# Loading the q weights ahead of the first K tile, and moving the first softmax ahead of a K tile's second turn

## The chip, the cores and the metric

The kernel runs on one core of one Trainium2 chip. The metric is the device time of one execution in microseconds (us); lower is better.

## The reference, cut to what matters

One decode step of a transformer block: layer norm, attention over the last 4096 positions of a cache (4 batches, 32 q heads on 16 K/V heads of width 128), output projection, then layer norm and a gated MLP.

```
q = xn @ wq                                  # 576 x 4096
scores = q @ K^T / sqrt(128);  p = softmax(scores);  o = p @ V
h = x + o @ wo;  h2 = h + (relu(gate) * up) @ W_down
```

K and V are 64 MB each in the window (a MB of a tile or of one load is 2^20 bytes here); with the weights 159.6 million bytes have to be read. There is little arithmetic per byte.

## The kernel before

K and V come in 16 tiles each, of 4 MB (128 partitions x 16384 bf16), into four slots of on-chip memory. One engine (SP) issues all these loads, in order. A load into a used slot first waits for the last reader of what lies there:

```python
def add_kv(kind, g):
    s = ring_slot(); off = slot0 + s * TILE
    place((kind, g), off, TILE, ("QK", g, 1) if kind == "K" else ("PV", g), ...)  # who must be done before the slot is reused
...
add_kv("K", 0)
place(("wq", 0), ...)            # q weights, a slot of their own; then 0.5 MB more of them
for g in range(1, NTILE):
    add_kv("K", g)
    if g >= 4:
        add_kv("V", g - 4)
```

So the queue is K0, wq, K1, K2, K3, K4, V0, K5, V1, K6, V2, K7 and so on. With four slots, K6 goes where K4 was: SP issues it when the scores of K4 are done.

A K tile is used in two halves. (QK stands for the matmuls that make the scores, PV for those of p @ V.) VectorE (DVE) turns a half (transposes it) in place, then TensorE (PE) makes 16 matmuls of 128x512 of it. There are two forms of the turn. The short form takes 4.4 us and its matmuls start every 0.43 us. The long form (`by_head`) takes 7.4 us and its matmuls start every 0.216 us at the full clock, 0.43 us at half of it.

```python
def do_k(g):                                  # after K4 the scores of batch 0 are complete
    if g: turn_k(g, 0)
    ...
    if g: turn_k(g, 1)
    if g == 4:
        row_max(0); pe_qk(g, 0, range(3)); head_max(0); pe_qk(g, 0, range(3, 4))
        exps(0); put_q(2)
    else:
        pe_qk(g, 0)
    ...                                       # g == 5: PV of V0 comes here
    pe_qk(g, 1)                               # frees the slot
```

Of the kernel before, what the change touches and what calls it, by code (L numbers as in the profile page):

```python
# [6 lines left out]
ALU = mybir.AluOpType  # L7
AX = mybir.AxisListType
# [12 lines left out]
NTILE = B * KVH // 4  # L21
# [6 lines left out]
BIG = 1e30  # L28


def by_head(g, w):
    return (g, w) in ((0, 0), (0, 1), (2, 1), (3, 1), (4, 1))


ENGS = ("sync", "scalar", "vector", "gpsimd", "tensor")
# [85 lines left out]
def bass_sequential_preLN__sliding_block_cached__glu_gated_reglu__decode_kernel(  # L121
# [12 lines left out]
    with ExitStack() as es:  # L134
# [7 lines left out]
        dve = lambda name, fn, deps=(): P.op("vector", name, fn, deps)  # L142
        act = lambda name, fn, deps=(): P.op("scalar", name, fn, deps)
        pool = lambda name, fn, deps=(): P.op("gpsimd", name, fn, deps)
# [6 lines left out]
        ident_f = sb("ident_f", [128, 128], FP32)  # L151
# [4 lines left out]
        c_am = sb("c_am", [128, 4, 16, 2], FP32)  # L156
# [5 lines left out]
        am = sb("am", [128, 4], FP32)  # L162
        msk = sb("msk", [128, 4], FP32)
# [75 lines left out]
        def add_kv(kind, g):  # L239
            b, qd = divmod(g, 4)  # L240
            s = ring_slot()
            off = slot0 + s * TILE
            cache = A_k_cache if kind == "K" else A_v_cache
            src = cache[b, 4 * qd:4 * qd + 4, SK - WIN:SK, :].rearrange("a (p t) d -> p a (t d)", p=32)
            place((kind, g), off, TILE, ("QK", g, 1) if kind == "K" else ("PV", g),
                  lambda e: e.dma_start(out=arena[:, off:off + TILE], in_=src), key=f"slot{s}")
# [5 lines left out]
        def last_rows(W):  # L252
            return W[512:576, :].rearrange("r (a n) -> (r a) n", a=2)

        add_kv("K", 0)
        s = ring_slot()
        wq_off = slot0 + s * TILE
        place(("wq", 0), wq_off, TILE, "QMM",
              lambda e: e.dma_start(out=arena[:, wq_off:wq_off + TILE], in_=main_rows(A_wq)), key=f"slot{s}")
        P.dma("sync", ("L", "wq", 1), lambda e: e.dma_start(out=pT[:, 0:2048], in_=last_rows(A_wq)), "d_wq1")  # L260
        for g in range(1, NTILE):
            add_kv("K", g)
            if g >= 4:
                add_kv("V", g - 4)
# [17 lines left out]
        for j in range(4):  # L282
            wd_off.append(off)
            for r0, r1 in ((0, 9),) if j < 3 else ((0, 6), (6, 9)):
                place(("wd", j, r0), off + r0 * D, (r1 - r0) * D, "DOWN",
                      lambda e, off=off, j=j, r0=r0, r1=r1: e.dma_start(  # L286
                          out=arena[:, off + r0 * D:off + r1 * D],
                          in_=B_W_down[j * 1152:(j + 1) * 1152, :].rearrange("(p r) n -> p (r n)", p=128)[:, r0 * D:r1 * D]))
# [5 lines left out]
                                                compare_op=ALU.not_equal, fill=1.0, base=0, channel_multiplier=1), ["c_idb0"])  # L294

        pool("c_xnT", lambda e: e.memset(xnT[:, :, :], 0.0))
        pool("c_idf0", lambda e: e.memset(ident_f[:, :], 0.0))
        pool("c_idf", lambda e: e.affine_select(out=ident_f[:, :], in_=ident_f[:, :], pattern=[[-1, 128]],
                                                compare_op=ALU.not_equal, fill=1.0, base=0, channel_multiplier=1), ["c_idf0"])
        pool("c_m40", lambda e: e.memset(c_m4[:, :, :], 0.0))  # L300
        pool("c_m41", lambda e: e.affine_select(out=c_m4[:, :, :], in_=c_m4[:, :, :], pattern=[[-1, 4], [-4, 32]],
                                                compare_op=ALU.not_equal, fill=1.0, base=0, channel_multiplier=1), ["c_m40"])
        pool("c_qW", lambda e: e.memset(arena[:, 0:2 * QWW].bitcast(FP32), 0.0))  # L303
        pool("c_am0", lambda e: e.memset(c_am[:, :, :, :], 0.0))
        pool("c_am1", lambda e: e.affine_select(out=c_am[:, :, :, :], in_=c_am[:, :, :, :], pattern=[[-2, 4], [-8, 16], [-1, 2]],
                                                compare_op=ALU.not_equal, fill=1.0, base=0, channel_multiplier=1), ["c_am0"])
# [7 lines left out]
                                                in_=c_qm[:, :, :].rearrange("p q (h j) -> p q h j", j=4),  # L314
# [20 lines left out]
        for q in range(4):  # L335
# [7 lines left out]
        dve("c_par0", lambda e: e.tensor_tensor(out=par[:, 0:1], in0=m4[:, 0:1], in1=m4[:, 2:3], op=ALU.add), ["c_m4"])  # L343
        dve("c_par", lambda e: e.tensor_scalar(out=par[:, 1:2], in0=par[:, 0:1], scalar1=-1.0, scalar2=1.0,
                                               op0=ALU.mult, op1=ALU.add), ["c_par0"])
        dve("c_am", lambda e: e.tensor_reduce(out=am[:, :], in_=c_am[:, :, :, :].rearrange("p a m s -> p a (m s)"), axis=AX.X, op=ALU.max),
            ["c_am1"])
        dve("c_msk", lambda e: e.tensor_scalar(out=msk[:, :], in0=am[:, :], scalar1=-1.0, scalar2=BIG, op0=ALU.add, op1=ALU.mult), ["c_am"])


        act("warm_sqrt", lambda e: e.activation(out=warm[:, 0:1], in_=eps_c[:, :], func=ACT.Sqrt), ["c_eps"])
# [64 lines left out]
        def put_q(b):  # L416
            for i in range(4):
                act(("QW", b), lambda e, i=i: e.copy(  # L418
                    out=bass.AP(tensor=arena, offset=32 * i * AW + b % 2 * QWW + 32 * i, ap=[[AW, 32], [128, 4], [514, 16], [1, 2]]),
                    in_=bass.AP(tensor=q_keep, offset=b * 128, ap=[[512, 32], [32, 4], [2, 16], [1, 2]])),  # L420
                    ["qkeep", "c_qW", ("QK", 4 * b - 5, 1) if b >= 2 else None] if i == 0 else [])


        def turn_k(g, w):
            k = arena[:, land[("K", g)] + w * QWW:][:, 0:QWW].bitcast(FP32)
            if by_head(g, w):
                dst = k.rearrange("p (n a k) -> p n k a", a=4, k=8)
                src = k.rearrange("p (n k a) -> p n k a", a=4, k=8)
            else:
                dst = k.rearrange("p (n h l a) -> p n l h a", h=2, l=2, a=2)  # L430
                src = k.rearrange("p (n l h a) -> p n l h a", h=2, l=2, a=2)
            dve(("TRA", g, w), lambda e: e.transpose(out=dst, in_=src), [("L", "K", g)] if w == 0 else [])  # L432


        def pe_qk(g, w, heads=range(4)):
            b, qd = divmod(g, 4)
            for a in heads:
                for cb in range(4):
                    first = a == cb == 0
                    deps = []  # L440
                    if first:
                        deps.append(("TRA", g, w))
                        if qd == 0 and w == 0:
                            deps.append(("QW", b))
                            if b >= 2:
                                deps += [("EXP", b - 2, 1), ("MAX", b - 2)]
                    sub, steps = (16 * a, [[2, 8]]) if by_head(g, w) else (a // 2 * 8 + a % 2 * 2, [[16, 4], [4, 2]])
                    off = land[("K", g)] + w * QWW + cb // 2 * 64 + sub + cb % 2
                    wo_ = b % 2 * QWW + (4 * qd + a) * 512 + cb * 128
                    pe(("QK", g, w), lambda e, off=off, steps=steps, wo_=wo_, qd=qd, first=first, last=a == cb == 3: e.matmul(  # L450
                        bank[SB[b % 2] + w], lhsT=arena[:, wo_:wo_ + 128],
                        rhs=bass.AP(tensor=arena, offset=off, ap=[[AW, 128], [128, 64]] + steps),
                        start=(qd == 0 and first), stop=(qd == 3 and last), skip_group_check=True), deps)
# [14 lines left out]
        def exps(b):  # L468
            pe(("MB", b), lambda e: e.matmul(m_ps[:, 0:1], lhsT=gm4[0:1, :], rhs=scl[0:1, 0:1], start=True, stop=True), [("GM1", b), "c_scl"])  # L469
            dve(("NB", b), lambda e: e.tensor_tensor(out=stat[:, b, 1:5], in0=msk[:, :],  # L470
                                                     in1=bass.AP(tensor=psb, offset=7 * 512, ap=[[4096, 128], [0, 4]]), op=ALU.add),
                [("MB", b), "c_msk"])
            for w in range(2):
                for a in range(4):
                    act(("EXP", b, w), lambda e, w=w, a=a: e.activation(  # L475
                        out=bass.AP(tensor=pp, offset=4096 + a // 2 * 2048 + w * 1024 + a % 2, ap=[[8192, 128], [2, 512]]),
                        in_=bank[SB[b % 2] + w], func=ACT.Exp,
                        bias=stat[:, b, 1 + a:2 + a], scale=SCALE, accum_out=stat[:, b, 5 + 4 * w + a:6 + 4 * w + a]),
                        [("NB", b), ("PTR", b - 1, 1) if b else "QT"] if a == 0 else [])
# [59 lines left out]

        pe_x()  # L540
        dve_x()
        turn_k(0, 0)
        turn_k(0, 1)
        pe_q()
        act_q()
        dve_q()
# [5 lines left out]
            ["c_s41", "c_sel0"])  # L552
        for q in range(4):
            dve("c_selc", lambda e, q=q: e.tensor_copy(out=selc[:, q, :, q], in_=e8[:, :]), ["c_e8", "c_selc0"])

        late = []

# [4 lines left out]
        def do_k(g):  # L562
            b, qd = divmod(g, 4)
            if g:
                turn_k(g, 0)
            if g == 5:
                turn_p(0, 0)
                turn_p(0, 1)
            flush()
            if g:  # L570
                turn_k(g, 1)
            if g == 4:
                row_max(0)
                pe_qk(g, 0, range(3))
                head_max(0)
                pe_qk(g, 0, range(3, 4))
                exps(0)
                put_q(2)
            else:
                pe_qk(g, 0)  # L580
            if g == 5:
                pe_pv(0)
            pe_qk(g, 1)
            if qd == 3 and g > 3:
                row_max(b)
# [153 lines left out]
```

## Time and profile before

| | before |
|---|---|
| time, median of 3 | 382.03 us (381.35 to 382.17) |
| bytes read | 159.6 million |
| share of the span that the 16 DMA engines spend on the main queue | 97.7% |
| DVE, PE busy | 59%, 73% |

The page of the profile. The first two rows are 40 equal slices of the span: busy tenths of the DMA engines, and the rate. The third row is the main load queue, with packets, MB and the share of the engines' time. The last is the chain of waits by line.

```profile
DMA  8999999999999999999999999999999999999993
GB/s 331 440 423 421 406 440 437 433 428 427 420 439 440 424 433 426 433 430 435 433 430 427 435 430 423 435 433 433 430 428 433 427 439 430 423 435 427 419 414 123
q1 hardware_dynamic: 6352, 159.59, 97.7%
PE psb L450 38%; DMA sb_arena<-in_A_k_cache_dram 19%; DVE sb_arena L432 11%; DMA sb_arena<-in_B_W_down_dram 9%; DMA sb_arena<-in_A_v_cache_dram 7%; PE psb L497 5%; POOL sb_arena L303 2%; ACT sb_pp L475 2%; DVE sb_o_sel L509 1%; DVE sb_o_tmp L505 1%; DVE sb_pp L484 1%; PE psb L534 0%; ACT sb_arena L418 0%; SPq L286 0%; PE psb L469 0%
```

The engines of the DMA are at work from the first slice to the last. The chain names PE, yet that is the wait of the next issue for its slot, and several megabytes are queued in front of that issue. The bound is loading.

The order of time of SP, 36 to 105 us: start, length, line, what is loaded.

```profile
40.09 1.18 SPq L246 DMA_DIRECT2D sb_arena<-in_A_k_cache_dram  x2
53.90 0.54 SPq L246 DMA_DIRECT2D sb_arena<-in_A_v_cache_dram  x1
64.27 0.53 SPq L246 DMA_DIRECT2D sb_arena<-in_A_k_cache_dram  x1
74.64 0.54 SPq L246 DMA_DIRECT2D sb_arena<-in_A_v_cache_dram  x1
88.36 0.54 SPq L246 DMA_DIRECT2D sb_arena<-in_A_k_cache_dram  x1
97.43 0.54 SPq L246 DMA_DIRECT2D sb_arena<-in_A_v_cache_dram  x1
```

These are K3 with K4, V0, K5, V1, K6 and V2. The trace also records each raise of a semaphore, the counter by which a transfer reports that it has landed. The Trainium skill, "DMA: Bandwidth & Descriptors", section "Why a DMA increments its semaphore by 16 and not by 1", says that a transfer runs on up to 16 engines that finish independently and the semaphore counts them. The trace agrees: 16 raises for each tile. I call the first of them the first landing. V1's first landing is at 91.96 us, so K6 was issued 3.6 us ahead of it. I call that the lead. In steady loading, one tile's first landing follows that of the tile before by 9.71 us, which is 432 GB/s.

The table by stretch (from:to, length, busy us and instructions of PE, PEld, DVE, ACT, POOL, then granted TensorE clock, DMA share, GB/s).

```profile
42.00:48.00 6.00, 6.00 (x15) 1.59 (x14) 3.77 (x2) 0.00 (x0) 0.00 (x0) 1.00 0.94 366
91.00:95.00 4.00, 4.00 (x11) 1.02 (x9) 4.00 (x2) 0.25 (x1) 0.00 (x0) 1.00 0.94 393
105.00:340.00 235.00, 176.11 (x892) 53.30 (x888) 136.37 (x91) 21.28 (x54) 0.00 (x0) 0.84 1.00 431
```

And the stretch at K4, first on DVE, then on PE, in order of time. A line merges instructions of one kind that follow each other (x is their number); brackets hold the idle time before it and what ended it.

```profile
68.14 11.71 DVE L432 STREAM_TRANSPOSE sb_arena<-sb_arena 128x4096 f32<-128x4096 f32 x2
79.70 1.17 DVE L457 TENSOR_REDUCE sb_stat<-psb 128x1 f32<-128x1024 f32 x1
83.67 0.16 DVE L470 TENSOR_TENSOR sb_stat<-sb_msk,psb 128x4 f32<-128x4 f32 x1 [1.77 <-PE psb L469]
```

```profile
74.45 5.34 PE L450 MATMUL psb<-sb_arena 128*128 128x512 bf16 x12
81.23 1.88 PE L450 MATMUL psb<-sb_arena 128*128 128x512 bf16 x4
83.56 11.99 PE L450 MATMUL psb<-sb_arena 128*128 128x512 bf16 x32
```

DVE turns both halves of K4 without a break (68.1 to 79.9). PE works on the first half meanwhile, and finds the second half turned when it gets there at 83.56. The last line merges the 16 matmuls of that half with 16 of K5. The 16 alone:

```profile
83.56 4.77 PE L450 MATMUL psb<-sb_arena 128*128 128x512 bf16 x16
```

### The profile page before, as it was taken

How to read it: one execution, taken by the hardware profiler on the slowest of the kernel's cores; microseconds unless marked ns; L12 is line 12 of the kernel's file. 1: busy time of each engine (PE TensorE's matmuls, PEld its weight loads, DVE VectorE, ACT ScalarE, POOL GpSimd, SP SyncE). 2: the span in 40 equal slices, each digit the busy share in tenths (PEclk: the TensorE clock that was granted, in tenths of full speed). 3: DMA queues.
4: the chain of work that ended last, by engine and by line, in shares of the span. 5: the costliest groups of instructions: out<-in, count | busy, mean ns of one | idle time of the engine just before them, and what ended most of it. 6: DMA issues, size and time to landing. Idle time of an engine off the chain costs nothing.

```text
span 381.1 us, 3671 instructions
## 1 busy us (share of the span) xinstructions
PE 278.0 (73%) x1629; PEld 92.8 (24%) x1629; DVE 223.2 (59%) x157; ACT 37.5 (10%) x95; POOL 16.3 (4%) x38
## 2 busy tenths in 40 slices
PE   0057999989959892979996939899969537036544
PEld 0013223322222221222221212222212213015322
DVE  0796799979383917965828279756464455002210
ACT  1112000015000006000000051000000340000100
POOL 8800000000000000000000000000000000000000
PEclk9998999989978897798997887989989956756687
DMA  8999999999999999999999999999999999999993
GB/s 331 440 423 421 406 440 437 433 428 427 420 439 440 424 433 426 433 430 435 433 430 427 435 430 423 435 433 433 430 428 433 427 439 430 423 435 427 419 414 123
DMA packets 6390, 159.81 MB, mean 419 GB/s; under 512 B 740, under 2 KB 744, under 8 KB 1384
## 3 DMA queue, kind: packets, MB, share of 16 engines
q1 hardware_dynamic: 6352, 159.59, 97.7%
q8 instruction: 12, 0.20, 0.2%
q14 instruction: 2, 0.02, 0.0%
q10 hardware_dynamic: 24, 0.01, 0.0%
HBM read 159.58 MB, written 0.00 MB: 419 GB/s over the span
## 4 chain that ended last, share of the span: by engine, by line
PE 44%; DMA 34%; DVE 15%; POOL 2%; ACT 2%; issue 1%; SPq 0%; POOLq 0%
PE psb L450 38%; DMA sb_arena<-in_A_k_cache_dram 19%; DVE sb_arena L432 11%; DMA sb_arena<-in_B_W_down_dram 9%; DMA sb_arena<-in_A_v_cache_dram 7%; PE psb L497 5%; POOL sb_arena L303 2%; ACT sb_pp L475 2%; DVE sb_o_sel L509 1%; DVE sb_o_tmp L505 1%; DVE sb_pp L484 1%; PE psb L534 0%; ACT sb_arena L418 0%; SPq L286 0%; PE psb L469 0%
## 5 line engine op out<-in xcount | busy, mean ns | idle before, releaser
L450 PE MATMUL psb<-sb_arena 128*128 128x512 bf16 x512 | 209.1, 578 | 10.5 <-DVE sb_arena L432 8.2
L432 DVE STREAM_TRANSPOSE sb_arena<-sb_arena 128x4096 f32<-128x4096 f32 x32 | 156.1, 4901 | 48.5 <-DMA sb_arena<-in_A_k_cache_dram 48.4
L450 PEld LDWEIGHTS psb<-sb_arena 128*128 128x128 bf16 x512 | 56.8, 114 | 153.6 <-issue 130.3
L497 PE MATMUL psb<-sb_arena,sb_pp 128*32 128x512 bf16 x512 | 35.9, 431 | 23.0 <-DMA sb_arena<-in_A_v_cache_dram 16.5
L475 ACT ACTIVATE sb_pp<-psb,sb_stat 128x512 bf16<-128x512 f32 x32 | 24.9, 847 | 247.8 <-DVE sb_stat L470 247.8
L505 DVE TENSOR_TENSOR sb_o_tmp<-psb,sb_qm 128x512 f32<-128x512 f32 x16 | 10.8, 676 | 27.9 <-PE psb L497 27.9
L497 PEld LDWEIGHTS psb<-sb_arena,sb_pp 128*32 128x32 bf16 x512 | 13.6, 106 | 47.9 <-issue 22.7
L457 DVE TENSOR_REDUCE sb_stat<-psb 128x1 f32<-128x1024 f32 x4 | 4.8, 1211 | 24.2 <-PE psb L450 24.2
L484 DVE STREAM_TRANSPOSE sb_pp<-sb_pp 128x2048 bf16<-128x2048 bf16 x8 | 18.0, 2278 | 1.4 <-ACT sb_pp L475 1.4
L509 DVE TENSOR_REDUCE sb_o_sel<-sb_o_tmp 128x128 f32<-128x512 f32 x16 | 16.6, 1037 | 0.6
L534 PE MATMUL psb<-sb_o_sel,sb_selw 128*32 128x32 f32 x128 | 2.4, 232 | 16.3 <-DVE sb_o_sel L509 16.3
L668 PE MATMUL psb<-sb_arena,sb_hnT 128*32 128x384 bf16 x120 | 7.9, 437 | 6.6 <-DMA sb_arena<-in_B_W_up_dram 4.5
L375 PE MATMUL psb<-sb_ident_b,sb_xn_bf 4*128 4x4 bf16 x4 | 0.3, 172 | 13.7 <-DVE sb_xnd_bf L364 13.7
L388 PE MATMUL psb<-sb_arena,sb_xnT 128*32 128x512 bf16 x32 | 3.6, 631 | 8.9 <-DMA sb_arena<-in_A_wq_dram 8.9
L675 DVE TENSOR_TENSOR sb_pp<-psb,sb_pp 128x384 bf16<-128x384 f32 x3 | 1.5, 551 | 12.6 <-PE psb L668 12.6
L517 PE MATMUL psb<-sb_stat,sb_sameh 128*128 128x1 f32 x8 | 1.8, 292 | 9.1 <-DVE sb_stat L515 9.1
L303 POOL MEMSET sb_arena<- 128x8192 f32 x1 | 6.9, 6925 | 0.0
L475 ACT ACTIVATION_READ_ACCUMULATOR sb_pp<-psb,sb_stat 128x1 f32 x32 | 6.6, 208 | 0.0
L668 PEld LDWEIGHTS psb<-sb_arena,sb_hnT 128*32 128x32 bf16 x120 | 4.2, 124 | 9.7 <-DMA sb_arena<-in_B_W_up_dram 4.8
L534 PEld LDWEIGHTS psb<-sb_o_sel,sb_selw 128*32 128x32 f32 x128 | 1.9, 142 | 17.4 <-DVE sb_o_sel L509 17.4
L701 PE MATMUL psb<-sb_arena,sb_pp 128*32 128x144 bf16 x144 | 3.8, 250 | 3.0 <-DMA sb_arena<-in_B_W_down_dram 2.5
L418 ACT COPY sb_arena<-sb_q_keep 32x128 bf16<-32x128 bf16 x16 | 4.8, 303 | 1.5 <-DVE sb_q_keep L409 1.4
(123 smaller groups left out, 71.9 us busy)
## 6 DMA issues: line engine op xcount, KB each, us to landing
sb_arena<-in_A_k_cache_dram SPq DMA_DIRECT2D x16, 4096.0 KB, 18.9
sb_arena<-in_A_v_cache_dram SPq DMA_DIRECT2D x16, 4096.0 KB, 24.2
sb_arena<-in_A_wo_dram SPq DMA_DIRECT2D x1, 4608.0 KB, 16.0
sb_arena<-in_B_W_gate_dram SPq DMA_DIRECT2D x1, 4608.0 KB, 30.9
sb_arena<-in_B_W_up_dram SPq DMA_DIRECT2D x1, 4608.0 KB, 42.3
sb_arena<-in_A_wq_dram SPq DMA_DIRECT2D x1, 4096.0 KB, 21.5
sb_arena<-in_B_W_down_dram SPq DMA_DIRECT2D x3, 1296.0 KB, 31.1
sb_arena<-in_B_W_down_dram SPq DMA_DIRECT2D x1, 864.0 KB, 32.7
```

Source lines behind the costliest of these rows:

```text
L303: pool("c_qW", lambda e: e.memset(arena[:, 0:2 * QWW].bitcast(FP32), 0.0))
L418: act(("QW", b), lambda e, i=i: e.copy(out=bass.AP(tensor=arena, offset=32 * i * AW + b % 2 * QWW + 32 * i, ap=[[AW, 32], [128, 4], [514, ...
L432: dve(("TRA", g, w), lambda e: e.transpose(out=dst, in_=src), [("L", "K", g)] if w == 0 else [])
L450: pe(("QK", g, w), lambda e, off=off, steps=steps, wo_=wo_, qd=qd, first=first, last=a == cb == 3: e.matmul(bank[SB[b % 2] + w], lhsT=aren ...
L457: dve(("MAX", b), lambda e: e.tensor_reduce(out=stat[:, b, 0:1], in_=s_ps, axis=AX.X, op=ALU.max, negate=True), [("QK", 4 * b + 3, 1)])
L475: act(("EXP", b, w), lambda e, w=w, a=a: e.activation(out=bass.AP(tensor=pp, offset=4096 + a // 2 * 2048 + w * 1024 + a % 2, ap=[[8192, 12 ...
L484: dve(("PTR", b, w), lambda e: e.transpose(out=dst, in_=src), [("EXP", b, w), ("PV", 4 * b - 1) if b else "QMM"])
L497: pe(("PV", g), lambda e, j=j, tq=tq, k=k: e.matmul(o_ps[32 * j:32 * j + 32, :], lhsT=pT[:, qd * 1024 + tq * 32:][:, 0:32], rhs=v[:, tq * ...
L505: dve(("OS", g), lambda e: e.tensor_tensor(out=o_tmp[:, :].rearrange("p (t d) -> p t d", t=4), in0=o_ps.rearrange("p (t d) -> p t d", t=4) ...
L509: dve(("OSEL", g), lambda e: e.tensor_reduce(out=o_sel[:, qd, :], in_=o_tmp[:, :].rearrange("p (t d) -> p d t", t=4), axis=AX.X, op=ALU.ad ...
L534: pe(("OT", b), lambda e, q=q, qd=qd: e.matmul(ot_ps[32 * qd:32 * qd + 32, 0:32], lhsT=selw[:, qd, 32 * q:32 * q + 32], rhs=o_sel[:, qd, 3 ...
L668: pe(("GU", g, c // 4), lambda e, g=g, m=m, j=j, lo=lo, c=c: e.matmul(bank[3 * g + m][32 * j:32 * j + 32, 0:384], lhsT=hnT[:, c if c < 4 e ...
```

## The change

Three parts are meant to take waits off PE and DVE at the start: (1) the q weights are loaded first and K0 second, (2) the q chain and its constants run before K0 is turned, and K0's first half uses the short turn, (3) the first softmax is no longer behind the turn of K4's second half.

```diff
 def by_head(g, w):
-    return (g, w) in ((0, 0), (0, 1), (2, 1), (3, 1), (4, 1))
+    return (g, w) in ((0, 1), (2, 1), (3, 1), (4, 1))
...
-        add_kv("K", 0)
         s = ring_slot()
         place(("wq", 0), wq_off, TILE, "QMM", ...)
-        for g in range(1, NTILE):
+        for g in range(NTILE):
             add_kv("K", g)
...   (the float identity and the mask constants move behind what the q chain needs)
         pe_x()
         dve_x()
-        turn_k(0, 0)
-        turn_k(0, 1)
         pe_q(); act_q(); dve_q(); put_q(0); put_q(1)
+        turn_k(0, 0)
+        turn_k(0, 1)
...
-            if g:
-                turn_k(g, 1)
             if g == 4:
                 row_max(0)
-                pe_qk(g, 0, range(3))
+                pe_qk(g, 0, range(1))
                 head_max(0)
-                pe_qk(g, 0, range(3, 4))
                 exps(0)
+                turn_k(g, 1)
+                pe_qk(g, 0, range(1, 4))
                 put_q(2)
             else:
+                if g:
+                    turn_k(g, 1)
                 pe_qk(g, 0)
```

More of the change, by code (lines that the diff above doesn't have):

```diff
@@ L296, in bass_sequential_preLN__sliding_block_cached__glu_gated_reglu__decode_kernel @@
         pool("c_xnT", lambda e: e.memset(xnT[:, :, :], 0.0))
-        pool("c_idf0", lambda e: e.memset(ident_f[:, :], 0.0))
-        pool("c_idf", lambda e: e.affine_select(out=ident_f[:, :], in_=ident_f[:, :], pattern=[[-1, 128]],
-                                                compare_op=ALU.not_equal, fill=1.0, base=0, channel_multiplier=1), ["c_idf0"])
         pool("c_m40", lambda e: e.memset(c_m4[:, :, :], 0.0))
@@ L303, in bass_sequential_preLN__sliding_block_cached__glu_gated_reglu__decode_kernel @@
         pool("c_qW", lambda e: e.memset(arena[:, 0:2 * QWW].bitcast(FP32), 0.0))
+        pool("c_idf0", lambda e: e.memset(ident_f[:, :], 0.0))
+        pool("c_idf", lambda e: e.affine_select(out=ident_f[:, :], in_=ident_f[:, :], pattern=[[-1, 128]],
+                                                compare_op=ALU.not_equal, fill=1.0, base=0, channel_multiplier=1), ["c_idf0"])
         pool("c_am0", lambda e: e.memset(c_am[:, :, :, :], 0.0))
@@ L345, in bass_sequential_preLN__sliding_block_cached__glu_gated_reglu__decode_kernel @@
                                                op0=ALU.mult, op1=ALU.add), ["c_par0"])
-        dve("c_am", lambda e: e.tensor_reduce(out=am[:, :], in_=c_am[:, :, :, :].rearrange("p a m s -> p a (m s)"), axis=AX.X, op=ALU.max),
-            ["c_am1"])
-        dve("c_msk", lambda e: e.tensor_scalar(out=msk[:, :], in0=am[:, :], scalar1=-1.0, scalar2=BIG, op0=ALU.add, op1=ALU.mult), ["c_am"])
         act("warm_sqrt", lambda e: e.activation(out=warm[:, 0:1], in_=eps_c[:, :], func=ACT.Sqrt), ["c_eps"])
@@ L541, in bass_sequential_preLN__sliding_block_cached__glu_gated_reglu__decode_kernel @@
         dve_x()
-        turn_k(0, 0)
-        turn_k(0, 1)
+        dve("c_am", lambda e: e.tensor_reduce(out=am[:, :], in_=c_am[:, :, :, :].rearrange("p a m s -> p a (m s)"), axis=AX.X, op=ALU.max),
+            ["c_am1"])
+        dve("c_msk", lambda e: e.tensor_scalar(out=msk[:, :], in0=am[:, :], scalar1=-1.0, scalar2=BIG, op0=ALU.add, op1=ALU.mult), ["c_am"])
         pe_q()
```

## The prediction

> **What bounds the kernel now.** Loading. The DMA row of the page stays at 90% or more in nearly every slice; the table by stretch gives 427 GB/s from 2.2 to 375.7 us, all 16 engines at work, and 159.6 MB have to come in. From 94 to 340 us the rate is 432 GB/s. The Trainium skill, "DMA: Bandwidth & Descriptors", section "Where 436 GB/s comes from", puts the ceiling at 435 GB/s; the trace agrees. About 370 us are bytes, 2 us come before the first packet and 4 us after the last landing (377.55 us). The change can only win where loading falters. The chain of waits names PE (38% on the QK line), but loads are queued so deep that this shows as waits of the issuing queue.
>
> **Where loading falters.** In 2 us bins it runs evenly up to 42 us. K3 is not issued before 40.09 us (it waits for both halves of QK0, which start at 31.35 behind wq landing at 22.96, the q chain and the copies of q). K2's landing begins at 43.1. Right then packets of 32 KB take 1.3 to 2.5 us instead of 1.21, and 42 to 48 us moves 366 GB/s instead of 432: 0.4 MB, about 0.9 us. A weaker dip, 401 GB/s at 90 to 94 us (about 0.3 us), follows K6's issue at 88.36, 3.1 us ahead of the end of V1.
>
> **What the change does.** wq lands at about 13 us, K0 at about 24. The ring gives K3 the slot of wq, free at about 18 us: K3 is queued over 20 us early and the dip at 42 to 48 should vanish, a gain of 0.7 to 0.9 us. The q chain ends by about 23 us, hidden. K0's first half turns in 4.45 us instead of 7.42, but QK there takes 0.43 us a matmul instead of 0.216 warm: QK0 runs from about 28.7 to 39.5, little better than the old 39.9. QK3 ends at about 74.2 (was 74.6).
> The softmax moves before the second turn of K4 (7.39 us). Row maximum about 74.3 to 75.5, exponentials 77.5 to 83.7 (was 83.8 to 90). But that turn now runs 77.5 to 84.9 (was 72.5 to 79.9), and QK of that half ends at about 88.5 to 90 (was 88.3). So K6 is issued 0 to 1.5 us later while V1 ends slightly earlier: its lead shrinks from 3.1 to 1 to 2.8 us, and the dip at 90 us may deepen, costing 0.2 to 1 us. From K5 on, the same order, shifted 0 to 1 us.
>
> **Sum.** 382.0 - 0.8 + 0.5 = 381.7 us; I say 381.6, 8 times in 10 between 380.3 and 383.3. Chances: faster by over 2% 0.01, within 2% 0.98, slower 0.01. 2% is 7.6 us, more than all the faltering.
>
> **What would show it.** Right: K3's issue at about 18 us; over 425 GB/s at 42 to 48 us; exponentials starting near 77.5 us; K6's issue at 88 to 90.5 us with a lead under 3 us; last weight landing at 376.5 to 378; the rate from 94 to 340 us unchanged. Wrong: K6's issue well before 88 us, a stop in loading of over 2 us, or a changed steady rate.
>
> **What would make it wrong.** A hole in loading at K6 as long as its lateness; a colder TensorE clock (idle from about 20 to 28.7 us and before QK4's second half) that delays the K tiles; instruction fetches, each of which holds one engine about 1 us, falling on an engine that is already last (landings of one transfer spread over 4.3 us at the end).

## More of the kernel before

A run has a profile (a trace of one execution) and several timed executions; the span of the profiled execution is 1 to 3 us shorter than its time, so times are compared with times and traces with traces.

## The result, and the profile after

| | before | changed |
|---|---|---|
| time, median of 4 | 381.79 us (381.35 to 382.17) | 383.66 us (382.91 to 384.01) |
| ratio | | 1.0046, 95% interval 1.0031 to 1.0062 |
| span of the profile | 381.1 us | 382.2 us |

A ratio is the mean time of one kernel's fast runs over that of the other's fast runs of the same rounds, so it is not quite the ratio of the medians. The change made the kernel slower, by about 0.5%: inside the 2% band, but clear of noise, and above the range that was predicted.

The page after: the same rows.

```profile
DMA  8999999998999999999999999999999999999993
GB/s 330 439 439 434 429 429 429 422 434 336 432 424 415 433 439 435 432 436 434 425 425 429 434 439 432 427 429 436 425 430 436 439 427 433 421 450 422 420 406 143
q1 hardware_dynamic: 6352, 159.59, 97.5%
```

One slice stands out: the tenth (86 to 95.5 us) moved 336 GB/s. The weak slices before it (406 at 38 to 48 us) are gone. SP in order of time:

```profile
39.56 0.54 SPq L246 DMA_DIRECT2D sb_arena<-in_A_k_cache_dram  x1
54.16 0.54 SPq L246 DMA_DIRECT2D sb_arena<-in_A_v_cache_dram  x1
64.53 0.54 SPq L246 DMA_DIRECT2D sb_arena<-in_A_k_cache_dram  x1
74.89 0.53 SPq L246 DMA_DIRECT2D sb_arena<-in_A_v_cache_dram  x1
91.79 0.54 SPq L246 DMA_DIRECT2D sb_arena<-in_A_k_cache_dram  x1
100.55 0.54 SPq L246 DMA_DIRECT2D sb_arena<-in_A_v_cache_dram  x1
```

K3 was issued at 16.79, outside this stretch, and K4 1.1 us earlier than before. V0, K5 and V1 go out within 0.3 us of their old times. K6 goes out at 91.79 instead of 88.36. V1's first landing was at 91.38, so the queue was already running empty. The table by stretch:

```profile
42.00:48.00 6.00, 6.00 (x16) 1.57 (x14) 5.60 (x2) 0.00 (x0) 0.00 (x0) 1.00 1.01 437
84.00:91.00 7.00, 5.48 (x14) 1.92 (x15) 7.00 (x3) 1.51 (x6) 0.00 (x0) 0.51 0.96 412
91.00:95.00 4.00, 4.00 (x12) 1.13 (x11) 4.00 (x3) 0.00 (x0) 0.00 (x0) 1.00 0.48 164
105.00:340.00 235.00, 178.49 (x898) 53.20 (x896) 137.05 (x91) 21.29 (x54) 0.00 (x0) 0.87 1.00 431
```

From 91 to 95 us the DMA engines worked 48% of the time. The rest of the kernel loads as before (431 GB/s from 105 to 340 us). At K4, DVE and then PE:

```profile
67.99 4.40 DVE L428 STREAM_TRANSPOSE sb_arena<-sb_arena 128x4096 f32<-128x4096 f32 x1
74.90 1.23 DVE L453 TENSOR_REDUCE sb_stat<-psb 128x1 f32<-128x1024 f32 x1 [2.51 <-PE psb L446]
77.96 0.16 DVE L466 TENSOR_TENSOR sb_stat<-sb_msk,psb 128x4 f32<-128x4 f32 x1 [0.47 <-PE psb L465]
78.03 11.69 DVE L428 STREAM_TRANSPOSE sb_arena<-sb_arena 128x4096 f32<-128x4096 f32 x2
```

```profile
77.85 5.34 PE L446 MATMUL psb<-sb_arena 128*128 128x512 bf16 x12
85.52 9.69 PE L446 MATMUL psb<-sb_arena 128*128 128x512 bf16 x24 [2.33 <-DVE sb_arena L428]
```

DVE now stands idle for 2.51 us until the scores of K3 are there for the row maximum, goes through the softmax's small steps, and only then starts the long turn of K4's second half (78.03 to 85.5, against 72.5 to 79.9 before; the line above merges it with the turn that follows, and PE's last line merges the second half with 8 matmuls of K5). PE runs dry for 2.33 us waiting for that turn. In the trace the granted clock then falls to 0.50 from 84.0 to 90.8 us: 12 of the 16 matmuls of K4's second half take 0.43 us each to the next instead of 0.216, so that half takes 6.1 us (85.5 to 91.6), 2.5 us more than the 3.6 us of the full clock and 1.3 us more than in the trace before the change, which had half the clock for 5 of them. Only then is K6 issued. Of the 3.4 us by which it goes out later, 2.0 are the later start of these matmuls (85.52 against 83.56) and the rest is that they took longer. The exponentials did start earlier, at 78.15 instead of 83.86 us, but nothing was waiting for them.

Where the tiles land (first of 16 / last of 16, us, from the trace's semaphore records). "Hole" is K6's first landing less V1's first landing less the usual 9.71.

| | K1 | V1 | K6 | hole | last weights |
|---|---|---|---|---|---|
| before | 33.39 / 33.96 | 91.96 / 93.66 | 101.66 / 103.37 | 0.0 | 373.20 / 377.55 |
| changed | 33.11 / 35.24 | 91.38 / 93.36 | 103.72 / 104.09 | 2.6 | 375.09 / 378.50 |

Up to V1 the changed kernel was 0.58 us ahead. It lost 2.6 us at K6 and never won them back.

### The profile page after: what moved, and what is told of

The parts are those of the page before. It is cut to its first block, busy times and chain, and to the rows that moved or that the text cites. A ratio compares the mean times of both kernels' runs of the same rounds, so it can differ in the third digit from the quotient of the medians.

```text
span 382.2 us, 3671 instructions
## 1 busy us (share of the span) xinstructions
PE 281.2 (74%) x1629; PEld 92.1 (24%) x1629; DVE 222.0 (58%) x157; ACT 37.5 (10%) x95; POOL 16.1 (4%) x38
## 4 chain that ended last, share of the span: by engine, by line
PE 47%; DMA 34%; DVE 15%; ACT 2%; SPq 1%; issue 1%
PE psb L446 40%; DMA sb_arena<-in_A_k_cache_dram 19%; DVE sb_arena L428 12%; DMA sb_arena<-in_B_W_down_dram 9%; DMA sb_arena<-in_A_v_cache_dram 7%; PE psb L493 5%; ACT sb_pp L471 2%; DVE sb_o_sel L505 1%; DVE sb_o_tmp L501 1%; DVE sb_pp L480 1%; PE psb L465 0%; PE psb L530 0%; SPq L285 0%; DVE sb_gm L459 0%; DVE sb_gm L461 0%
## 5 line engine op out<-in xcount | busy, mean ns | idle before, releaser
L446 PE MATMUL psb<-sb_arena 128*128 128x512 bf16 x512 | 212.6, 585 | 22.2 <-DVE sb_arena L428 22.1
L428 DVE STREAM_TRANSPOSE sb_arena<-sb_arena 128x4096 f32<-128x4096 f32 x32 | 152.8, 4804 | 48.0 <-DMA sb_arena<-in_A_k_cache_dram 48.0
L668 PE MATMUL psb<-sb_arena,sb_hnT 128*32 128x384 bf16 x120 | 9.0, 483 | 6.6 <-DMA sb_arena<-in_B_W_up_dram 4.5
```

What stands on the lines that cost most here:

```text
L428: dve(("TRA", g, w), lambda e: e.transpose(out=dst, in_=src), [("L", "K", g)] if w == 0 else [])
L446: pe(("QK", g, w), lambda e, off=off, steps=steps, wo_=wo_, qd=qd, first=first, last=a == cb == 3: e.matmul(bank[SB[b % 2] + w], lhsT=aren ...
L668: pe(("GU", g, c // 4), lambda e, g=g, m=m, j=j, lo=lo, c=c: e.matmul(bank[3 * g + m][32 * j:32 * j + 32, 0:384], lhsT=hnT[:, c if c < 4 e ...
```

## The experiments

Theory A: the third part alone costs the time, because it delays the scores of K4's second half, so that K6 is issued after the queue has drained. Rival B: the new loading order costs it. Inside A there are two causes of the delay to tell apart: the place of the turn and the half clock.

### The change without its third part

```diff
+            if g:
+                turn_k(g, 1)
             if g == 4:
                 row_max(0)
-                pe_qk(g, 0, range(1))
+                pe_qk(g, 0, range(3))
                 head_max(0)
+                pe_qk(g, 0, range(3, 4))
                 exps(0)
-                turn_k(g, 1)
-                pe_qk(g, 0, range(1, 4))
                 put_q(2)
```

> The change without its third part: wq first, K0 second, K0's new turn; the softmax of the first batch stays behind K4's second turn, as before. Theory A (the softmax move delays QK of K4's second half, K6 is issued only when V1 has drained, loading has a hole of about 2.6 us): K6 issued at about 88 us, no hole at 91 to 93 us, landings of K6 and later about 0.5 us earlier than in the kernel before; time 380.9 to 381.6 us, ratio to before 0.998 to 1.000. Rival B (the new loading order costs the time, by its own pattern of packets or by a later K0): the time stays at about 383.5 us, ratio 1.004 to 1.006.

Measured: 381.18 us, before 381.71; ratio 0.9989 (0.9977 to 1.0001). SP and the table by stretch of this run:

```profile
86.69 0.53 SPq L246 DMA_DIRECT2D sb_arena<-in_A_k_cache_dram  x1
96.97 0.54 SPq L246 DMA_DIRECT2D sb_arena<-in_A_v_cache_dram  x1
```

```profile
91.00:95.00 4.00, 4.00 (x10) 0.91 (x8) 4.00 (x2) 0.00 (x0) 0.00 (x0) 1.00 1.08 467
```

K6 goes out at 86.69, the hole is gone (K6 lands first at 101.18, 9.71 after V1), and the time is below that of the kernel before. In this trace the clock was full from 34.4 to 109.5 us, so the matmuls of K4's second half ran from 83.03 to K6's issue in 3.7 us. Rival B falls: the new loading order, together with the second part, costs nothing.

### The third part alone, on the kernel before

The edit is the last block of the change's diff.

> The kernel before with the third part alone. Theory A: K6 issued at 91.5 to 92 us, V1 drained by 92; hole of 2 to 2.6 us, time 383.8 to 384.4 us, ratio 1.005 to 1.007. Rival B: as before, ratio 0.999 to 1.001.

Measured: 383.41 us; ratio 1.0044 (1.0026 to 1.0062). SP:

```profile
92.50 0.54 SPq L246 DMA_DIRECT2D sb_arena<-in_A_k_cache_dram  x1
```

K6 was issued at 92.50, V1 first landed at 91.77, and the hole was 3.0 us. The time is a little under what was expected (383.8), the interval of the ratio reaches its lower end. The third part carries the loss by itself.

### Keeping the clock up while PE waits

```diff
                 turn_k(g, 1)
                 pe_qk(g, 0, range(1, 4))
+                for _ in range(12):      # thrown away; the next PV starts this bank anew
+                    pe("FILL", lambda e: e.matmul(bank[2][:, :], lhsT=ident_b[:, :], rhs=arena[:, QWW:QWW + 512], start=True, stop=True, ...))
                 put_q(2)
```

> The changed kernel with 12 idle-filling matmuls (result thrown away, into a bank that the next PV overwrites) between QK of K4's first half and the wait for its second turn, 82.9 to 85.5 us in the trace. They tell apart two causes of the late K6 inside theory A. If the half clock (0.50 from 84 to 90.6 us) is what takes it from late to too late: QK of K4's second half takes about 3.6 us instead of 6.3, K6 is issued at about 89 us, 2.3 us ahead of the drain, most of the hole goes, time 381.3 to 382.2 us, ratio 0.999 to 1.002. If only the order of the turns matters: K6 still at 91 us or later, time 383 us or more, ratio 1.004 or more.

Measured: 382.58 us; ratio 1.0024 (1.0012 to 1.0036). PE in order of time:

```profile
83.21 3.15 PE L577 MATMUL psb<-sb_arena,sb_ident_b 128*128 128x512 bf16 x12
86.20 3.62 PE L446 MATMUL psb<-sb_arena 128*128 128x512 bf16 x16
89.98 7.07 PE L446 MATMUL psb<-sb_arena 128*128 128x512 bf16 x16 [0.16 <-DVE sb_arena L428]
```

The 16 matmuls took 3.62 us instead of 6.1, K6 was issued at 89.85, with a lead of 1.6 us, and the hole shrank from 2.6 to 0.7 us. The time fell by about half of the loss, not by nearly all of it: it missed the expected 381.3 to 382.2. So the half clock accounts for about 1.9 us of K6's delay. Against the version without the third part (86.69) 3.2 us are left, with the place of the turn; about 0.5 of them are the filling itself, which ran on after the turn had ended (85.67). These shares rest on one trace, whose clock differed from that of the changed kernel already before the filling (half from 80.6 to 84.0 us).

### The short turn for K4's second half

```diff
 def by_head(g, w):
-    return (g, w) in ((0, 1), (2, 1), (3, 1), (4, 1))
+    return (g, w) in ((0, 1), (2, 1), (3, 1))
```

> The changed kernel with K4's second half turned by the short form (4.4 us instead of 7.4; its QK then takes 0.43 us a matmul at either clock, 6.9 us in all). The turn ends at about 82.5 us, before QK of the first half does, so PE does not idle and QK of the second half ends at about 89.9: K6 issued 1.5 us ahead of the drain, as in the run with the filling matmuls. Theory A: hole 0.5 to 1 us, time 382.0 to 382.8 us, ratio 1.001 to 1.003. If the place of the softmax costs by itself, whatever K6's issue does: ratio 1.004 or more.

Measured: 382.02 us, before 381.94; ratio 1.0004 (0.9990 to 1.0017). SP:

```profile
90.03 0.54 SPq L246 DMA_DIRECT2D sb_arena<-in_A_k_cache_dram  x1
```

K6 was issued at 90.03, a lead of 1.5 us; the hole was 0.9 us. The softmax stands where the change put it, and the loss against the kernel before is gone within the interval. Against the version without the third part 0.6 to 0.8 us are left (by the ratios and by the medians), about the hole: no cost of the softmax's place shows except through K6's issue.

### K6 loaded in two halves

The first half of K6 waits only for the scores of K4's first half; compute is untouched.

```diff
+            if kind == "K" and g == 6:
+                for w in range(2):
+                    place((kind, g, w), off + w * QWW, QWW, ("QK", g, w), ..., key=f"half{s}_{w}")
...
+            if (kind, g) == ("K", 4):      # first half of the slot is free after QK of the first half
+                for blk in range(off // 64, (off + QWW) // 64): owner[blk] = ("QK", g, 0)
```

> The changed kernel, with K6 loaded as two transfers of 2 MB: the first waits only for QK of K4's first half (done at about 83 us), the second for its second half, as before (about 91.8). Compute order, clock and all else stay as changed. Theory A: the first half is issued at about 83 us and keeps the engines at work to about 96 us, no hole at 91.7 to 93.1 us; time 380.9 to 381.8 us, ratio 0.998 to 1.001. If the time were lost by PE or DVE being late for anything else than issuing K6: it stays at about 383.5 us, ratio 1.004 or more.

Measured: 381.99 us; ratio 1.0008 (0.9993 to 1.0022), just above the expected time and clearly below the changed kernel. SP, then the table by stretch:

```profile
83.33 9.20 SPq L248 DMA_DIRECT2D sb_arena<-in_A_k_cache_dram  x2
100.75 0.54 SPq L253 DMA_DIRECT2D sb_arena<-in_A_v_cache_dram  x1
```

```profile
91.00:95.00 4.00, 4.00 (x12) 1.18 (x11) 4.00 (x3) 0.00 (x0) 0.00 (x0) 0.98 1.02 434
101.00:105.00 4.00, 4.00 (x11) 1.08 (x10) 3.61 (x4) 0.00 (x0) 0.00 (x0) 1.00 0.75 274
```

There is no hole at 91 to 95 us. In this trace a part of it came back one load later: V2 waits for PV of V0, which was just as late as in the changed kernel (issued 100.75), and K6 now landed in time (101.17), so V2's lead was 0.4 us and the hole 1.95 us. In the changed kernel the hole at K6 had hidden that. The trace is of the slowest of the six executions (383.14 us; the others took 381.21 to 382.53), so it does not show how large V2's hole was in the others.

### K6 held back on purpose

On the first experiment's kernel: K6 waits for the scores of K5's first half, 8 us more, and no instruction of PE, DVE or ACT moves in the program.

```diff
+            if (kind, g) == ("K", 4):
+                for blk in range(off // 64, (off + TILE) // 64): owner[blk] = ("QK", 5, 0)
```

> The run without the softmax move, with K6 held back on purpose: it waits for QK of K5's first half (ends at about 95.0 us) instead of QK of K4's second half (86.7), V1 drains from 91.5 on. Compute order is untouched. Theory A, simple form (every us of hole in the issue is a us of time): hole about 4.8 us, time 381.2 + 4.8 = 386 us, ratio 1.011. Theory A with catching up (the end is set by the last of the 16 engines, which is some 1.5 us behind the first by then and uses the hole to catch up): the first engine loses 4.8 us, the time only about 3.3: 384.5 us, ratio 1.007. Rival (a hole before 100 us is made good later, so the softmax move costs through something else): below 382 us.

Measured: 386.97 us, before 381.94; ratio 1.0135 (1.0121 to 1.0149). SP and the table by stretch:

```profile
95.69 0.54 SPq L246 DMA_DIRECT2D sb_arena<-in_A_k_cache_dram  x1
```

```profile
91.00:95.00 4.00, 4.00 (x10) 1.02 (x9) 4.00 (x2) 0.44 (x2) 0.00 (x0) 1.00 0.04 16
95.00:101.00 6.00, 6.00 (x43) 1.78 (x42) 2.18 (x1) 0.00 (x0) 0.00 (x0) 1.00 0.65 262
```

A hole in the issue alone, with compute as it was, costs time: the third possibility, that a hole early in the kernel is made good later, falls. Both expected sizes were too small because the hole was 6.6 us, not 4.8: K6 went out 0.7 us later than assumed (95.69 against 95.0), and I had counted too little for the restart of the queue (below). The ratio is 1.46% above that of the run it is built on, about 5.6 us, less than the 6.6 us of the first landings. That would fit the second form (the last engine catches up during a hole), but in the profiled pair the last engine ended 6.6 us later as well (382.43 against 375.87), the times of the two profiled executions differ by 6.8 us (387.72 against 380.96), and the intervals reach half a us to each side. It stays open whether a hole costs a little less than its length.

### All K tiles in halves, to beat both kernels

The first experiment's kernel, with every K tile loaded as two transfers with a semaphore each, the first one released by the scores of the old tile's first half.

> A version meant to beat both: wq first and K0 second, the softmax where it was, and every K tile loaded as two transfers of 2 MB, each with its own semaphore, the first released by QK of the old tile's first half. If the dips that are left come from short leads of the queue: K transfers issued 5 us or more earlier than in the run without the softmax move, time 380.8 to 381.3 us, ratio 0.997 to 0.9995. If the smaller packets (16 KB) cost more than the leads bring, or no dip is left to win: the same as that run within its interval, or up to 1 us more.

Measured: 382.4 us; ratio 1.0011 (0.9998 to 1.0024). The K loads went out earlier (K6's halves at 78.73 and 82.61), but there was no dip left to win, and a K tile in two halves took 9.79 us from first landing to first landing instead of 9.71. Sixteen tiles at 0.08 us are 1.3 us, an estimate that covers the 1 us by which this version lies above the one it was built on. It is no improvement.

### The changed kernel and the version without the third part, once more

Both unedited, on one chip.

> The changed kernel once more, unedited, on the same chip as the next run. Theory A and the first measurement: 383.2 to 384.0 us, ratio 1.003 to 1.006. If the first measurement was a matter of the chip or the hour: ratio below 1.002.

> The change without the softmax move once more, to narrow its interval and to compare it directly with the changed kernel: 381.0 to 381.4 us, ratio 0.998 to 0.9995, about 2.2 us below the changed kernel. If its earlier lead on the kernel before was chance: ratio 0.9995 to 1.001.

Measured: the changed kernel 383.49 us, ratio 1.0027 (1.0010 to 1.0045), just under the expected 1.003; without the third part 381.29 us, ratio 0.9980 (0.9967 to 0.9992); before 381.75 us. The two differ by 2.2 us, as expected. The version with only the first two parts is faster than the kernel before by 0.2% here (0.1% in its first run, where the interval reached 1), and it beats both.

The second trace of the changed kernel is useful for itself. Its SP and its table by stretch:

```profile
90.88 0.54 SPq L246 DMA_DIRECT2D sb_arena<-in_A_k_cache_dram  x1
```

```profile
84.00:91.00 7.00, 5.47 (x17) 2.05 (x18) 7.00 (x3) 1.53 (x6) 0.00 (x0) 0.76 0.96 412
```

While K4's second half ran, the same program had half the clock only from 85.6 to 89.0 us this time, one step of the clock's record of 3.4 us instead of two (0.76 against 0.51 in this stretch). K6 went out 0.9 us sooner and the hole was 1.6 us instead of 2.6. The Trainium skill, "TensorE: Matmul & The Clock Gate", section "Part 1: The HAM clock gate (the "warmup" mystery)", describes a clock that is halved after an idle window of about 3.4 us, with windows that run free of the program, so that cold matmuls vary from run to run. These two traces agree with the step of 3.4 us and with cold matmuls that vary from run to run; whether the window has to be idle is another matter (last section). That this is why the changed kernel's times scatter more (382.2 to 384.0) than those of the version without the third part (381.0 to 381.9) is likely, but not shown.

### All holes together

The lead is the first landing of the transfer before, less the start of the issue of the next. The times are medians; all else, with the span, is from the one trace of each run, in us:

| run | next load | lead | hole | lead + hole | span of the trace | time |
|---|---|---|---|---|---|---|
| without third part | K6 | 4.8 | 0.0 | | 379.2 | 381.18 |
| before | K6 | 3.6 | 0.0 | | 381.1 | 381.71 |
| warm fill | K6 | 1.6 | 0.7 | 2.3 | 380.7 | 382.58 |
| short turn | K6 | 1.5 | 0.9 | 2.4 | 380.5 | 382.02 |
| changed, second time | K6 | 0.6 | 1.6 | 2.3 | 381.5 | 383.49 |
| K6 in halves | V2 | 0.4 | 1.95 | 2.4 | 381.1 | 381.99 |
| changed | K6 | -0.4 | 2.6 | 2.2 | 382.2 | 383.66 |
| third part alone | K6 | -0.7 | 3.0 | 2.3 | 382.9 | 383.41 |
| K6 held back | K6 | -4.3 | 6.6 | 2.3 | 385.9 | 386.97 |

The sum is 2.2 to 2.4 us in all seven: here a load of 4 MB had to be issued about 2.3 us before the first engine landed the one before, or the difference was lost. The line is not sharp to a few tenths. V2, issued 2.9 to 3.3 us ahead in five of these traces, still lost 0.02 to 0.19 us; K3 lost 0.27 us at a lead of 3.0 in the kernel before and nothing at a lead of 2.1 in the third part alone (issued at 41.10, K2's first landing at 43.22).

Compared as trace with trace, the spans lie within 0.9 us of 379.2 plus the hole, but for the kernel before, which lies 1.9 us above. The first landing of the last weights, which leaves out the spread of the 16 engines at the end, follows the hole within 0.6 us in all nine (372.58 without the third part). The median times lie within 1.2 us of 381.2 plus the hole. (The time of the kernel before is that of the first call of experiments; in the others it was 381.75 to 381.94. Which execution its trace belongs to is not on record.)

## Why the prediction was wrong, point by point

- **The bound.** Right. Loading bounds the kernel; the rate from 105 to 340 us was 431 GB/s before and after, and what moved the time in the experiments was when loads were issued.
- **"The dip at 42 to 48 should vanish, a gain of 0.7 to 0.9 us."** K3's early issue and the full rate came as predicted (issued at 16.79, 437 GB/s in that stretch), but the size was read from the wrong view. Rates of a few us count packets of 32 KB by their start, and 16 engines start them nearly together: without any hole the stretch 91 to 95 us shows 393 in one run and 467 in another. In landings, K3 came 9.98 us after K2 before the change, against the usual 9.71: 0.27 us in that trace. That the late issue cost them is not shown: in the trace of the third part alone K3 went out later still, the stretch showed 382 GB/s, and K3 landed 9.71 us after K2. Another 0.3 us, which the prediction did not have, were there from K1 on (33.39 against 33.11; 33.51 in the other trace of the old order, 33.08 to 33.26 in the eight of the new order that load K1 whole). The first packet of 32 KB starts at 1.76 us instead of 2.15, which fits that gain; the issue of the q weights takes 0.42 us where K0's took 0.63, and that this is its cause is argued, not shown. Together 0.58 us at V1, and 0.5 us in the time of both runs without the third part.
- **The turn and the exponentials.** Right within 0.7 us: exponentials from 78.15 (predicted 77.5), the long turn from 78.03 to 85.5 (77.5 to 84.9).
- **"QK of that half ends at about 88.5 to 90." This is the step that failed.** It ended at 91.6. From the end of the turn the prediction left 3.6 to 5.1 us for the 16 matmuls (84.9 to 88.5 or 90); they took 6.1, because 12 of them ran at half clock, and the turn ended 0.6 us later than predicted. The prediction named a colder clock before just these matmuls as a risk and left it out of the sum. The warm fill showed the term: 3.62 us for the same matmuls, K6 issued 1.9 us sooner.
- **"Its lead shrinks from 3.1 to 1 to 2.8 us, and the dip at 90 us may deepen, costing 0.2 to 1 us."** The lead was -0.4 us and the cost 2.6 us. The lead failed, by the step above. (The prediction counted it to the end of V1's packets; its 3.1 is 3.6 by the measure used here, so its 1 to 2.8 is about 1.5 to 3.3.) The price within those leads did not fail: in the warm fill, where the matmuls ran at the full clock, K6 went out at 89.85, the lead was 1.6, the hole 0.7 and the time 382.58 us, all inside the prediction's ranges (though not its sum: it was to be 0.3 us below the kernel before, and the warm fill was 0.9 us above). What it had no term for is a lead below 1.5; the experiments give about 2.3 us, less the lead, as the price there.
- **The sum.** -0.8 + 0.5 was predicted; in landings it was -0.6 + 2.6, about +2 us, and +1.9 us was measured.
- **"A stop in loading of over 2 us"** was named as what would show the reasoning wrong, and it is what happened: by first landings the hole was 2.6 us.

What stays open: whether the last engine catches up in a hole (in the main pair the first landing of the last weights came 1.9 us later, the last landing 0.95 us later); and why K3 and some V2 loads lost up to 0.27 us at leads above 2.3 us.

## What to carry to other kernels

When loading bounds a kernel, read every change of order as a change of when the next load is issued: follow the slot back to the instruction that frees it, and compare its end with the landing of the load before, not with the engine's idle time. Moving work forward on one engine moves something else back; here the softmax that nobody waited for delayed the matmuls that free a slot, and most of those matmuls then ran at half the clock, for which the pause it put into TensorE is the likely reason (the filling matmuls took it away). Measure the parts of a change one by one: two parts of this one helped by 0.1 to 0.2%, and the third cost 0.4 to 0.6%.

## What the Trainium skill lacked or had wrong

- "DMA: Bandwidth & Descriptors" gives a first-byte latency of about 0.6 us for loads issued from SP ("Latency and other measured facts") and fits a fixed cost of about 2.0 us for a DMA of the other, software path ("Anatomy of one DMA"). It does not say how far ahead a load must be issued in a saturated queue. The runs show 2.2 to 2.4 us before the first landing of the load before, for seven 4 MB loads, with exceptions of a few tenths of a us. In the changed kernel the first packet started 1.3 us after the start of K6's issue (91.79 to 93.1), and the first packets after the hole took about 2 us instead of 1.21.
- The same page gives no price for splitting a large load in a queue that is never empty. Here two loads of 2 MB took 9.79 us where one of 4 MB took 9.71.
- "TensorE: Matmul & The Clock Gate", Part 1, ties the half clock in its table of states to an idle window of about 3.4 us and gives no share of busy time at which the clock falls. In the changed kernel the clock fell at 84.0 us after 3.4 us in which PE was busy for 2.59 us (before the change: at 82.5, after 3.4 us with 2.26 us busy). So by the busy time of the trace, which is modelled for PE, a window need not be idle throughout. That share alone does not decide either: before the change the clock stayed full at 324.8 us after 3.4 us with 1.4 us busy.
- "Runtime: NRT & Kernel Launch", section "Instruction fetch mechanics", calls the cost of fetching instructions mostly hidden. In these traces each fetch of 16 KB holds one of the 16 DMA engines for about 1 us, 12 times in the kernel before, and by the end the landings of one transfer lie 4.3 us apart (373.20 to 377.55). That the fetches make that spread is argued from their times, not shown by a run.
